# Fetching the output-projection matrix in runs of four rows per partition, with the attention output permuted to match

## Chip, cores, metric

One Trainium2 chip, one core. The metric is device time of one execution in microseconds (us). Repeated executions differ by up to 1.4 us in all (370.9 to 372.3 for the kernel before, in 11 runs of one set), so differences below 1 us need several rounds.

Names used below: PE is TensorE (matrix multiplies), DVE is VectorE, ACT is ScalarE, POOL is GpSimd, and SP is SyncE, which here issues loads. PSUM is the memory that PE writes to; `arena` is the kernel's one large SBUF buffer. A load is cut into packets, which 16 DMA engines carry.

## The reference

A gated sum of two branches on eight tokens: attention of one query position over a window of 2,048 cached positions, then an output projection, and a two-layer MLP.

```python
g = sigmoid((x * gate_w).sum(-1, keepdims=True))
q = (x @ wq).reshape(B, 1, 32, 128)                 # B = 8, D = 576
k, v = k_cache[:, :, -2048:], v_cache[:, :, -2048:] # 16 kv heads, each used by 2 query heads
o = softmax(q k^T / sqrt(128)) v
a = o.reshape(B, 1, 4096) @ wo                      # wo is 4096 x 576, bf16: 4.7 MB
b = gelu(layernorm(x) @ w1 + b1) @ w2 + b2          # F = 4608
out = g * a + (1 - g) * b
```

Keys and values are 134 MB of the 154 MB that must be read. `wo` is 3% of it.

## The kernel before

A plan of operations with dependencies is put in order once for each engine, on the host, and then emitted. SP issues nearly all loads into nine slots of 16 KB per partition. A key tile is transposed on DVE and multiplied on PE; a value tile goes straight to PE. After every eight query heads, one load brings the eight blocks of 128 rows of `wo` that belong to them. Row p of a block goes to partition p, so each partition gets eight separate runs of one row, 576 x 2 = 1,152 B.

```python
def wo_chunk(i):                                   # i = 0..3, eight heads each
    s = take_slot()
    h0 = WO_CH * i                                 # WO_CH = 8
    dst = slot(s)[:, 0:WO_CH * WOP].rearrange("p (t c) -> p t c", t=WO_CH)      # WOP = 768
    d = dma("sp", lambda e: e.dma_start(dst[:, :, 0:D],
            A_wo[128 * h0:128 * (h0 + WO_CH), :].rearrange("(t p) c -> p t c", p=128)), ...)
    for item in range(h0 // 2, (h0 + WO_CH) // 2):
        mms = [(oT[:, item, h, :], dst[:, 2 * item + h - h0, 0:D]) for h in range(2)]
        ops.append(AccGroup("proj%d" % item, mms, [oT_done[item], d], cost=0.5).op)
    ...
# AccGroup: for each (lhsT, rhs) two matmuls of 288 columns, added up in one PSUM bank.
# ... cut ...
stream += [("B", 0)] + [("M", i) for i in range(FC)]   # after the last wo load: b2, then w2 in four parts
def m2_chunk(ci):                                      # w2: 1296 KB a part, the last one in three pieces
    cuts = [0, 4, 7, 9] if ci == FC - 1 else [0, FJ]
    # ... cut ...
```

Of the kernel before, what the change touches and what calls it, by code (L numbers as in the profile page):

```python
# [6 lines left out]
BF = mybir.dt.bfloat16  # L7
F32 = mybir.dt.float32
ACTF = mybir.ActivationFunctionType
# [29 lines left out]
class _Plan:  # L39
# [10 lines left out]
    def add(self, eng, fn, deps=(), name=None, cost=0.1, after=(), prio=0):  # L50
        op = _Op(eng, fn, deps, name, cost, after=after, prio=prio)
        op.idx = len(self.all)
        self.all.append(op)
        return op

    def dma(self, eng, fn, semkey, nbytes, deps=(), name=None, after=(), prio=0):
        op = _Op(eng, fn, deps, name, self.DMA_ISSUE, after=after, is_dma=True, dma_sem=semkey, nbytes=nbytes, prio=prio)
        op.idx = len(self.all)
        self.all.append(op)
        return op  # L60
# [111 lines left out]
def build_kernel(nc, A_x, A_k_cache, A_v_cache, A_wq, A_wo, B_x, B_w1, B_b1, B_w2, B_b2, gate_w, out):  # L172
    B, Sq, D = A_x.shape
# [12 lines left out]
    FC, FJ = 4, 9  # L186
    FT = FC * FJ
    FCW = 128 * FJ
    WOP = 768
    NJ = 2  # L190
    WO_CH = 8
    JN = D // NJ
# [4 lines left out]
    with ExitStack() as es:  # L197
# [5 lines left out]
        def req(name, nelem, dt, align=64):  # L203
            sz = 2 if dt == BF else 4
            o = aoff[0] + ARENA_BASE
            o = (o + align - 1) // align * align - ARENA_BASE
            R[name] = (o, nelem, dt)
            aoff[0] = o + nelem * sz
# [34 lines left out]
        req("rg", 2 * 32, F32)  # L243
        req("o32", 2 * 16, F32)
        req("oT", Hkv * 16, BF)
        req("out_sb", JN, BF)
        req("PT", 2 * 2048, BF)
        req("P", 2048, BF)
# [11 lines left out]
        arena = es.enter_context(nc.sbuf_tensor("arena", [128, (aoff[0] + 1) // 2], BF))  # L260
        AST = _pst(arena)
        arena_f = arena.bitcast(F32)

        def aoffs(name):
            return R[name][0] // 2
# [4 lines left out]
        def view(name, parts=128):  # L270
            o, n, dt = R[name]
            a = arena[0:parts, o // 2: o // 2 + (n * (2 if dt == BF else 4)) // 2]
            if dt == F32:
                a = a.bitcast(F32)
            return a

        ident = view("ident")
        ones_bf = view("ones_bf")
        ones_f = view("ones_f")
# [20 lines left out]
        dsum = view("dsum")  # L300
# [2 lines left out]
        o32 = view("o32").rearrange("p (u m) -> p u m", u=2)  # L303
        oT = view("oT").rearrange("p (u h b) -> p u h b", u=Hkv, h=2)
        out_sb = view("out_sb")
        PT = view("PT").rearrange("p (g r m) -> p g r m", g=2, m=32)
        Pm = view("P")
        RAW = view("RAW")
# [6 lines left out]
        def slot(s):  # L315
            return RAW[:, s * SE:(s + 1) * SE]
# [7 lines left out]
        def col(i, parts=128):  # L324
# [3 lines left out]
        ps = es.enter_context(nc.psum_tensor("ps", [128, 8, 512], F32))  # L328
        PST = _pst(ps)
# [2 lines left out]
        BK_OS = (4, 5)  # L332
        BK_S = 6
        BK_ACC = 7

        eng_sems = {e: es.enter_context(nc.semaphore("sem_" + e)) for e in ENGS}
        dma_keys = ["x", "b", "b2", "wq", "w1", "out", "outb"] + ["s%d" % i for i in range(NSLOT)] + ["t%d" % i for i in range(4)]
# [3 lines left out]
        add, dma = P.add, P.dma  # L341
# [4 lines left out]
        o_ident = add("pool", lambda e: e.affine_select(out=ident, in_=ones_bf[:, 0:128], pattern=[[-1, 128]], compare_op=ALU.is_equal,  # L346
                                                        fill=0.0, base=0, channel_multiplier=1), deps=[o_ones], name="ident", cost=0.3)
# [33 lines left out]
        for s in range(2):  # L381
            o_xz.append(add("dve", (lambda s=s: lambda e: e.tensor_copy(xz[:, s, :].rearrange("p (k z) -> p k z", z=2)[:, :, s], x_sb[:, 512:576]))(),  # L382
                            deps=dx + [o_xz0], name="xz%d" % s, cost=0.12))
# [12 lines left out]
        for s in range(2):  # L396
            o_yz.append(add("dve", (lambda s=s: lambda e: e.tensor_copy(yz[:, s, :].rearrange("p (k z) -> p k z", z=2)[:, :, s], y_bf[:, 512:576]))(),
                            deps=[o_y, o_yz0], name="yz%d" % s, cost=0.12))
# [30 lines left out]
        def b1ev_fn(e):  # L429
# [5 lines left out]
                   deps=[o_dga, o_dgb, o_onesf], name="g_pe", cost=0.4, after=[o_yTp])  # L435
        o_yT = add("dve", ev_T(yT, 1), deps=[o_gp, o_yTp], name="yT_ev", cost=0.2)
        o_gb = add("dve", lambda e: e.tensor_copy(gb, ps[:, BK_X, 384:400]), deps=[o_gp], name="gb_ev", cost=0.15)
# [118 lines left out]
        exp_done, pt_done, pv_last = {}, {}, {}  # L556
        rg_done = {}
        o_item_ev = {}
        proj_ops = {}
        oT_done = {}  # L560

        def src_of(cache, g, q):
# [8 lines left out]
        def softmax(g):  # L571
            k = lambda i, n=1, parts=128, p0=0: sm[p0:p0 + parts, g, i:i + n]
            MX, GA, GB_, GC_, M01, M23, TT, NB, SUM, S = 0, 1, 2, 3, 4, 5, 6, 7, 8, 12
            mx = add("dve", lambda e: e.tensor_reduce(out=k(MX), in_=ps[:, 0:4, :].rearrange("p a n -> p (a n)"), axis=AXL.X, op=ALU.max), deps=[qk_unit[4 * g + 3]], name="mx%d" % g, cost=2.25, prio=5)  # L574
            sh = []
            for i, dst in ((1, GA), (2, GB_), (3, GC_)):
                sh.append(add("dve", (lambda i=i, dst=dst: lambda e: e.tensor_copy(k(dst, 1, 32), k(MX, 1, 32, 32 * i)))(), deps=[mx], name="mg%d_%d" % (g, i), cost=0.16, prio=5))  # L577
            m01 = add("dve", lambda e: e.tensor_tensor(out=k(M01, 1, 32), in0=k(MX, 1, 32), in1=k(GA, 1, 32), op=ALU.max), deps=[sh[0]], name="m01_%d" % g, cost=0.16, prio=5)
            m23 = add("dve", lambda e: e.tensor_tensor(out=k(M23, 1, 32), in0=k(GB_, 1, 32), in1=k(GC_, 1, 32), op=ALU.max), deps=sh[1:], name="m23_%d" % g, cost=0.16, prio=5)
            tt = add("dve", lambda e: e.tensor_tensor(out=k(TT, 1, 32), in0=k(M01, 1, 32), in1=k(M23, 1, 32), op=ALU.max), deps=[m01, m23], name="t_%d" % g, cost=0.16, prio=5)  # L580
            nbs = []
            for q in range(4):
                nbs.append(add("dve", (lambda q=q: lambda e: e.tensor_scalar(out=k(NB, 1, 32, 32 * q), in0=k(TT, 1, 32), scalar1=-SCALE, scalar2=None, op0=ALU.mult))(),  # L583
                               deps=[tt], name="nb%d_%d" % (g, q), cost=0.16, prio=5))
            exs = []
            for c in range(4):
                def fn(e, c=c):
                    return e.activation(out=Pm[:, 512 * c:512 * c + 512], in_=ps[:, c, :], func=ACTF.Exp, bias=k(NB), scale=SCALE, accum_out=k(SUM + c))  # L588
                exs.append(add("act", fn, deps=nbs + ([pt_done[g - 1][c]] if g else [o_xg, o_zz]), name="exp%d_%d" % (g, c), cost=0.9, prio=5))
            exp_done[g] = exs  # L590
            pts = []
            for c in range(4):
                pts.append(add("dve", (lambda c=c: lambda e: e.transpose(PT[:, g % 2, 16 * c:16 * c + 16, :].rearrange("p r m -> p (r m)"), Pm[:, 512 * c:512 * c + 512]))(),  # L593
                               deps=[exs[c]] + ([pv_last[g - 2]] if g >= 2 else [o_yTp, o_b1p]), name="pt%d_%d" % (g, c), cost=0.62, prio=5))
            pt_done[g] = pts
            s_ = add("dve", lambda e: e.tensor_reduce(out=k(S), in_=k(SUM, 4), axis=AXL.X, op=ALU.add), deps=exs, name="s_%d" % g, cost=0.16, prio=5)
            ds = add("dve", lambda e: e.tensor_scalar(out=dsum, in0=i32, scalar1=k(S), scalar2=None, op0=ALU.mult), deps=[s_] + o_i32 + ([rg_done[g - 1]] if g else []), name="ds_%d" % g, cost=0.16, prio=5)
            sp_ = add("pe", lambda e: e.matmul(ps[:, BK_S, 0:32], ones_f, dsum, start=True, stop=True), deps=[ds, o_yT, o_gb], name="sum_pe%d" % g, cost=0.5, prio=5)  # L598
            rc = add("dve", lambda e: e.reciprocal(out=rr, in_=ps[:, BK_S, 0:32]), deps=[sp_], name="rc_%d" % g, cost=0.16, prio=5)  # L599

            def rg_fn(e):
                in1 = bass.AP(arena_f, offset=foffs("gb"), ap=[[AST // 2, 128], [0, 2], [1, 8], [0, 2]])
                return e.tensor_tensor(out=rg[:, g % 2, :].rearrange("p (l b h) -> p l b h", l=2, b=8), in0=rr.rearrange("p (l b h) -> p l b h", l=2, b=8), in1=in1, op=ALU.mult)
            deps = [rc, o_gb]
            if g >= 2:
                deps.append(oT_done[2 * (g - 2) + 1])
            rg_done[g] = add("dve", rg_fn, deps=deps, name="rg_%d" % g, cost=0.16, prio=5)
# [81 lines left out]
        def wo_chunk(i):  # L689
            s = take_slot()  # L690
            h0 = WO_CH * i
            dst = slot(s)[:, 0:WO_CH * WOP].rearrange("p (t c) -> p t c", t=WO_CH)
            d = dma("sp", lambda e: e.dma_start(dst[:, :, 0:D], A_wo[128 * h0:128 * (h0 + WO_CH), :].rearrange("(t p) c -> p t c", p=128)),
                    "s%d" % s, WO_CH * 128 * D * 2, deps=slot_free[s], name="d_wo%d" % i, after=last_dma[-1:])
            last_dma.append(d)
            ops = []
            for item in range(h0 // 2, (h0 + WO_CH) // 2):
                mms = [(oT[:, item, h, :], dst[:, 2 * item + h - h0, 0:D]) for h in range(2)]
                ops.append(AccGroup("proj%d" % item, mms, [oT_done[item], d], cost=0.5).op)
            slot_free[s] = ops  # L700

        o_m2 = []
# [105 lines left out]
```

## Time and profile before

| | before |
|---|---|
| time, median of the first 3 runs | 372.0 us (371.48 to 372.11) |
| load queue, share of 16 DMA engines | 98.5% |
| PE / DVE / ACT / POOL busy | 65 / 57 / 8 / 10% |
| instruction fetches (queue 8) | 24, of 16,384 B each |

These are lines of the profile page of the kernel before. "DMA" gives the mean busy share of the 16 DMA engines in 40 equal slices, in tenths. The queue lines (q1, q8) give packets, megabytes, and share of the 16 engines' span. The line that starts with "DMA 6" is the chain of waits by engine. The last line is the issue of the projection loads: KB each, and us from issue to landing.

```profile
span 369.5 us, 7044 instructions
...
DMA  8999999999999999999999999999999999999994
...
DMA packets 14934, 154.77 MB, mean 419 GB/s; under 512 B 1292, under 2 KB 5428, under 8 KB 6072
...
q1 hardware_dynamic: 14848, 154.29, 98.5%
q8 instruction: 24, 0.39, 0.4%
...
DMA 63%; PE 20%; DVE 13%; SPq 2%; issue 1%; DVEq 0%
...
arena<-in_A_wo_dram SPq DMA_DIRECT2D x4, 1152.0 KB, 37.3
```

DMA is at 9 tenths everywhere but at the ends, so DMA engine time is what counts. PE, DVE and ACT have room.

How the rate sags where a projection load runs (208 to 212 us), against a stretch without one. The columns of this view: stretch; length; busy us (instructions) of PE, PE weight loads, DVE, ACT, POOL; granted clock; DMA share; GB/s.

```profile
208.00:212.00 4.00, 0.00 (x0) 0.00 (x1) 3.74 (x9) 2.78 (x8) 0.00 (x0) 0.68 0.98 383
150.00:196.00 46.00, 32.64 (x401) 17.95 (x406) 28.05 (x29) 3.16 (x11) 4.58 (x22) 0.80 1.01 430
```

383 GB/s against 430, at the same DMA share: small packets carry less.

The end of the kernel before, from its timeline: start us, duration us, engine, line, operation; in brackets the idle time before it and who ended it.

```profile
350.83 1.87 PE L663 MATMUL ps<-arena 128*128 128x8 bf16 x64 [2.97 <-DMA arena<-in_A_v_cache_dram]
352.74 0.23 DVE L685 TENSOR_TENSOR arena<-ps,arena 128x16 bf16<-128x16 f32 x1 [13.97 <-PE ps L663]
...
353.93 2.65 PE L530 MATMUL ps<-arena 128*8 128x288 bf16 x20 [1.23 <-DMA arena<-in_A_wo_dram]
...
357.10 2.33 PE L530 MATMUL ps<-arena 128*8 128x288 bf16 x18 [0.51 <-DMA arena<-in_B_w_dram]
...
360.06 2.33 PE L530 MATMUL ps<-arena 128*8 128x288 bf16 x18 [0.63 <-DMA arena<-in_B_w_dram]
...
363.15 3.96 PE L530 MATMUL ps<-arena 128*8 128x288 bf16 x36 [0.77 <-DMA arena<-in_B_w_dram]
```

L663 is the last value tile, L685 scales the attention output, and L530 holds the projection and then the second MLP layer. Each L530 line from 353.93 on begins when weights land: `wo` at 353.9, then three parts of `w2`; PE ends at 367.1.

The trace holds a record of each DMA packet: queue, size, start, duration. These durations are the same from the 5th to the 95th percentile (for the 256 packets of 4,608 B in the kernel before, 181 ns at the 95th):

| packet | duration in the record | from one packet's start to the next one's on the same engine |
|---|---|---|
| 1,152 B (`wo`) | 51 ns | 47 ns |
| 4,608 B | 178 ns | 174 ns |
| 16,384 B (K, V) | 611 ns | 607 ns |

### The profile page before, as it was taken

To read this page: it belongs to the slowest core of one execution; us is meant where nothing else is said; L and a number is where in the kernel's file an instruction comes from. 1 tells how busy PE (TensorE), PEld (TensorE's weight loads), DVE (VectorE), ACT (ScalarE), POOL (GpSimd) and SP (SyncE) were. 2 spreads that over 40 slices of the span, in tenths; PEclk is the share of its full clock that TensorE was granted. 3 is DMA by queue.
4 is the path that set the end of the run, shared out by engine and by line. 5 is a ranking of instruction groups with operands and counts; after the bars stand their busy time and mean duration, and the time that the engine had idled before them with its cause. 6 is when DMAs were issued, how large, how long until landed. Compare 5 with 4: busy or idle time off the path is not lost.

```text
span 369.5 us, 7044 instructions
## 1 busy us (share of the span) xinstructions
PE 242.0 (65%) x3089; PEld 137.5 (37%) x3117; DVE 210.0 (57%) x253; ACT 28.6 (8%) x85; POOL 37.5 (10%) x163
## 2 busy tenths in 40 slices
PE   0349983896695486663965395755767385783376
PEld 0339430454242243232523243432424243343343
DVE  0704699688694663459744764478544964464000
ACT  1010001100300200003000300003000300003000
POOL 7030010011011001000101010100101000000000
PEclk9999998799698879686898879696957788785556
DMA  8999999999999999999999999999999999999994
GB/s 343 426 422 424 427 432 431 434 424 431 429 431 429 413 436 427 429 427 429 435 426 429 414 431 432 431 431 426 426 435 433 418 424 427 435 429 426 413 420 167
DMA packets 14934, 154.77 MB, mean 419 GB/s; under 512 B 1292, under 2 KB 5428, under 8 KB 6072
## 3 DMA queue, kind: packets, MB, share of 16 engines
q1 hardware_dynamic: 14848, 154.29, 98.5%
q8 instruction: 24, 0.39, 0.4%
q14 instruction: 6, 0.05, 0.0%
q10 hardware_dynamic: 56, 0.03, 0.0%
HBM read 154.31 MB, written 0.01 MB: 418 GB/s over the span
## 4 chain that ended last, share of the span: by engine, by line
DMA 63%; PE 20%; DVE 13%; SPq 2%; issue 1%; DVEq 0%
DMA arena<-in_A_k_cache_dram 42%; PE ps L641 12%; DMA arena<-in_B_w_dram 11%; DMA arena<-in_A_v_cache_dram 10%; DVE arena L627 9%; PE ps L663 3%; DVE arena L574 2%; PE ps L487 2%; SPq L716 1%; PE ps L530 1%; PE ps L637 1%; SPq L657 1%; PE ps L489 1%; DVE arena L577 0%; DVE arena L593 0%
## 5 line engine op out<-in xcount | busy, mean ns | idle before, releaser
L627 DVE STREAM_TRANSPOSE arena<-arena 128x2048 f32<-128x2048 f32 x64 | 145.0, 2296 | 79.1 <-DMA arena<-in_A_k_cache_dram 74.6
L641 PE MATMUL ps<-arena 128*128 128x512 bf16 x491 | 144.6, 449 | 45.1 <-DVE arena L627 44.0
L641 PEld LDWEIGHTS ps<-arena 128*128 128x128 bf16 x512 | 52.5, 109 | 129.2 <-DVE arena L627 53.2
L663 PE MATMUL ps<-arena 128*128 128x8 bf16 x2048 | 56.4, 166 | 12.3 <-DMA arena<-in_A_v_cache_dram 12.3
L663 PEld LDWEIGHTS ps<-arena 128*128 128x128 bf16 x2048 | 56.1, 97 | 19.1 <-DMA arena<-in_A_v_cache_dram 14.2
L620 POOL COPY arena<-arena 32x32 bf16<-32x32 bf16 x128 | 26.0, 203 | 177.2 <-PE ps L641 162.6
L637 PE MATMUL ps<-arena 128*128 128x512 bf16 x25 | 12.3, 630 | 40.2 <-DVE arena L593 36.7
L588 ACT ACTIVATE arena<-ps,arena 128x512 bf16<-128x512 f32 x32 | 21.5, 685 | 107.4 <-DVE arena L583 107.4
L574 DVE TENSOR_REDUCE arena<-ps 128x1 f32<-128x2048 f32 x8 | 18.3, 2282 | 17.7 <-PE ps L641 17.7
L593 DVE STREAM_TRANSPOSE arena<-arena 128x512 bf16<-128x512 bf16 x32 | 19.9, 675 | 0.9 <-ACT arena L588 0.9
L637 PEld LDWEIGHTS ps<-arena 128*128 128x128 bf16 x32 | 3.5, 128 | 42.9 <-DVE arena L593 38.5
L530 PE MATMUL ps<-arena 128*8 128x288 bf16 (+1 forms) x140 | 14.7, 377 | 3.1 <-DMA arena<-in_B_w_dram 1.9
L685 POOL TENSOR_TENSOR arena<-arena 128x16 bf16<-128x16 f32 x15 | 4.0, 265 | 121.2 <-ACT arena L678 121.2
L678 ACT ACTIVATE arena<-ps 128x16 f32<-128x16 f32 x15 | 2.8, 184 | 170.2 <-PE ps L663 170.2
L487 PE MATMUL ps<-arena 128*128 128x8 bf16 x144 | 10.9, 201 | 4.6 <-DMA arena<-in_B_w_dram 4.6
L487 PEld LDWEIGHTS ps<-arena 128*128 128x128 bf16 x144 | 10.8, 160 | 5.0 <-DMA arena<-in_B_w_dram 5.0
L530 PEld LDWEIGHTS ps<-arena 128*8 128x8 bf16 (+1 forms) x140 | 7.1, 106 | 10.9 <-DMA arena<-in_B_w_dram 3.6
L599 DVE RECIPROCAL arena<-ps 128x32 f32<-128x32 f32 x8 | 2.9, 358 | 11.4 <-PE ps L598 11.4
L409 PE MATMUL ps<-arena 8*128 8x8 bf16 x8 | 0.5, 167 | 13.4 <-DVE arena L382 9.7
L734 DVE CAST arena<-ps 8x288 bf16<-8x288 f32 x1 | 0.4, 446 | 14.3 <-PE ps L530 14.3
L685 DVE TENSOR_TENSOR arena<-ps,arena 128x16 bf16<-128x16 f32 x1 | 0.2, 228 | 14.0 <-PE ps L663 14.0
L489 PE MATMUL ps<-arena 128*128 128x8 bf16 x36 | 7.2, 201 | 0.0
(79 smaller groups left out, 79.4 us busy)
## 6 DMA issues: line engine op xcount, KB each, us to landing
arena<-in_A_k_cache_dram SPq DMA_DIRECT2D x32, 2048.0 KB, 34.0
arena<-in_A_v_cache_dram SPq DMA_DIRECT2D x32, 2048.0 KB, 34.4
arena<-in_B_w_dram SPq DMA_DIRECT2D x1, 4608.0 KB, 24.2
arena<-in_A_wo_dram SPq DMA_DIRECT2D x4, 1152.0 KB, 37.3
arena<-in_A_wq_dram SPq DMA_DIRECT2D x1, 4096.0 KB, 13.0
arena<-in_B_w_dram SPq DMA_DIRECT2D x3, 1296.0 KB, 14.8
arena<-in_B_w_dram SPq DMA_DIRECT2D x2, 576.0 KB, 20.5
arena<-in_A_wq_dram SPq DMA_DIRECT2D x1, 512.0 KB, 3.6
```

The source lines that it names most:

```text
L487: ins = e.matmul(out_, lhsT, yT[:, kt, :], start=(kt == 0), stop=False)
L489: ins = e.matmul(out_, lhsT, yT[:, 4 + c // 2, :], start=False, stop=True)
L530: ins = e.matmul(ps[32 * j:32 * j + 8, BK_ACC, 0:JN], lhsT, rhs[:, JN * j:JN * j + JN], start=False, stop=True, skip_group_check=True, til ...
L574: mx = add("dve", lambda e: e.tensor_reduce(out=k(MX), in_=ps[:, 0:4, :].rearrange("p a n -> p (a n)"), axis=AXL.X, op=ALU.max), deps=[qk_ ...
L588: return e.activation(out=Pm[:, 512 * c:512 * c + 512], in_=ps[:, c, :], func=ACTF.Exp, bias=k(NB), scale=SCALE, accum_out=k(SUM + c))
L593: pts.append(add("dve", (lambda c=c: lambda e: e.transpose(PT[:, g % 2, 16 * c:16 * c + 16, :].rearrange("p r m -> p (r m)"), Pm[:, 512 * ...
L620: return e.tensor_copy(dst, src)
L627: tr = add("dve", (lambda h=h, kb=kb: lambda e: e.transpose(bass.AP(arena_f, offset=foffs("KT") + kb * 2048, ap=[[AST // 2, 128], [1, 2048]]),
L637: mm = e.matmul(ps[:, rc, :], maskL, maskR, start=True, stop=False)
L641: mm = e.matmul(ps[:, rc, :], qbd[:, ub, 2 * h + ee, :], rhs, start=False, stop=(q == 3 and h == 1 and ee == 1))
L663: mm = e.matmul(ps[:, BK_OS[item % 2], 8 * (q % 2):8 * (q % 2) + 8], slot(s)[:, r * 128:(r + 1) * 128], PT[:, g % 2, r, 8 * q:8 * q + 8], ...
L685: return e.tensor_tensor(out=oT[:, item, :, :].rearrange("p h b -> p b h"), in0=src_.rearrange("p (b h) -> p b h", h=2), in1=rg[:, g % 2, ...
```

## The change

The intent is to have fewer, longer DMA packets. Partition p takes four rows of `wo` that are neighbours in memory, 4p to 4p+3 of a group of 512 rows (four heads): one run of 4,608 B. The contraction on PE needs the attention output's rows on the same partitions. So for each load 16 matmuls with columns of the identity select and place them, and ACT copies the result from PSUM. The number of projection matmuls stays. Followed by hand, the indices pair each row of `wo` with its head and position. The cut parts of the diff put the permutation and the softmax sum, which share a PSUM bank, in order.

```diff
-    dst = slot(s)[:, 0:WO_CH * WOP].rearrange("p (t c) -> p t c", t=WO_CH)
-    d = dma("sp", lambda e: e.dma_start(dst[:, :, 0:D], A_wo[...].rearrange("(t p) c -> p t c", p=128)), ...)
+    dst = slot(s)[:, 0:WO_CH * D]
+    d = dma("sp", lambda e: e.dma_start(dst.rearrange("p (g n) -> p g n", g=2),
+            A_wo[...].rearrange("(g p t) c -> p g (t c)", g=2, t=4)), ...)
+    def perm_fn(e):
+        for hh in range(4):
+            rhs = bass.AP(arena, offset=aoffs("oT") + 8 * (h0 + hh), ap=[[AST, 128], [32, 2], [1, 8]])
+            for t in range(4):
+                out_ = bass.AP(ps, offset=32 * hh * PST + BK_S * 512 + WC + 8 * t, ap=[[PST, 32], [32, 2], [1, 8]])
+                lhsT = bass.AP(arena, offset=aoffs("ident") + t, ap=[[AST, 128], [4, 32]])
+                mm = e.matmul(out_, lhsT, rhs, start=True, stop=True, skip_group_check=True, tile_position=(0, 32 * hh))
+        return mm
+    pm = add("pe", perm_fn, deps=[oT_done[h0 // 2 + k] for k in range(4)] + ..., name="perm%d" % i, cost=1.0)
+    pe_ = add("act", lambda e: e.activation(out=w8, in_=ps[:, BK_S, WC:WC + 64], func=ACTF.Copy), deps=[pm] + ...)
-    for item in range(h0 // 2, (h0 + WO_CH) // 2):
-        mms = [(oT[:, item, h, :], dst[:, 2 * item + h - h0, 0:D]) for h in range(2)]
-        ops.append(AccGroup("proj%d" % item, mms, [oT_done[item], d], cost=0.5).op)
+    for n in range(2):
+        mms = [(w8[:, 8 * c:8 * c + 8], dst[:, c * D:(c + 1) * D]) for c in range(4 * n, 4 * n + 4)]
+        ops.append(AccGroup("proj%d_%d" % (i, n), mms, [pe_, d], cost=1.0).op)
```

More of the change, by code (lines that the diff above doesn't have):

```diff
@@ L188, in build_kernel @@
     FCW = 128 * FJ
-    WOP = 768
     NJ = 2
@@ L245, in build_kernel @@
         req("oT", Hkv * 16, BF)
+        req("wo8", 2 * 64, BF)
         req("out_sb", JN, BF)
@@ L305, in build_kernel @@
         out_sb = view("out_sb")
+        wo8 = view("wo8").rearrange("p (u n) -> p u n", u=2)
         PT = view("PT").rearrange("p (g r m) -> p g r m", g=2, m=32)
@@ L334, in build_kernel @@
         BK_ACC = 7
+        WC = 128
         eng_sems = {e: es.enter_context(nc.semaphore("sem_" + e)) for e in ENGS}
@@ L558, in build_kernel @@
         o_item_ev = {}
-        proj_ops = {}
+        b6_w, b6_r = [], [o_yT, o_gb]
+        wo_ops = {}
         oT_done = {}
@@ L597, in softmax @@
             ds = add("dve", lambda e: e.tensor_scalar(out=dsum, in0=i32, scalar1=k(S), scalar2=None, op0=ALU.mult), deps=[s_] + o_i32 + ([rg_done[g - 1]] if g else []), name="ds_%d" % g, cost=0.16, prio=5)
-            sp_ = add("pe", lambda e: e.matmul(ps[:, BK_S, 0:32], ones_f, dsum, start=True, stop=True), deps=[ds, o_yT, o_gb], name="sum_pe%d" % g, cost=0.5, prio=5)
+            sp_ = add("pe", lambda e: e.matmul(ps[:, BK_S, 0:32], ones_f, dsum, start=True, stop=True), deps=[ds] + b6_r[-2:], after=b6_w[-1:], name="sum_pe%d" % g, cost=0.5, prio=5)
+            b6_w.append(sp_)
             rc = add("dve", lambda e: e.reciprocal(out=rr, in_=ps[:, BK_S, 0:32]), deps=[sp_], name="rc_%d" % g, cost=0.16, prio=5)
+            b6_r.append(rc)
             def rg_fn(e):
@@ L691, in wo_chunk @@
             h0 = WO_CH * i
-            dst = slot(s)[:, 0:WO_CH * WOP].rearrange("p (t c) -> p t c", t=WO_CH)
-            d = dma("sp", lambda e: e.dma_start(dst[:, :, 0:D], A_wo[128 * h0:128 * (h0 + WO_CH), :].rearrange("(t p) c -> p t c", p=128)),
+            dst = slot(s)[:, 0:WO_CH * D]
+            d = dma("sp", lambda e: e.dma_start(dst.rearrange("p (g n) -> p g n", g=2), A_wo[128 * h0:128 * (h0 + WO_CH), :].rearrange("(g p t) c -> p g (t c)", g=2, t=4)),
                     "s%d" % s, WO_CH * 128 * D * 2, deps=slot_free[s], name="d_wo%d" % i, after=last_dma[-1:])
             last_dma.append(d)
+            def perm_fn(e):
+                mm = None
+                for hh in range(4):
[5 more added lines that the diff above has]
+                return mm
+            pm = add("pe", perm_fn, deps=[oT_done[h0 // 2 + k] for k in range(4)] + [o_ident] + b6_r[-2:], after=b6_w[-1:], name="perm%d" % i, cost=1.0)
+            b6_w.append(pm)
+            w8 = wo8[:, i % 2, :]
+            pe_ = add("act", lambda e: e.activation(out=w8, in_=ps[:, BK_S, WC:WC + 64], func=ACTF.Copy), deps=[pm] + wo_ops.get(i - 2, []), name="pev%d" % i, cost=0.25, prio=3)
+            b6_r.append(pe_)
             ops = []
-            for item in range(h0 // 2, (h0 + WO_CH) // 2):
-                mms = [(oT[:, item, h, :], dst[:, 2 * item + h - h0, 0:D]) for h in range(2)]
-                ops.append(AccGroup("proj%d" % item, mms, [oT_done[item], d], cost=0.5).op)
+            for n in range(2):
+                mms = [(w8[:, 8 * c:8 * c + 8], dst[:, c * D:(c + 1) * D]) for c in range(4 * n, 4 * n + 4)]
+                ops.append(AccGroup("proj%d_%d" % (i, n), mms, [pe_, d], cost=1.0).op)
+            wo_ops[i] = ops
             slot_free[s] = ops
```

## The prediction

> **What bounds the kernel now.** The DMA engines. The page's slice table shows DMA at 9 tenths in all slices but the first and last; the queue table puts the load queue at 98.5% of the 16 engines' span (154.29 MB, 14,848 packets). In the chain of waits DMA is 63%. Loads are issued about 34 us before they land (DMA issues table), so work is always queued. PE (65%) and DVE (57%) are not at their limit. What counts is DMA engine time, plus the short tail after the last landing.
>
> **What the change removes.** Each of the four projection loads (1152 KB) is 1,024 packets of 1,152 B. The trace's packet records give 51 ns for 1,152 B, 178 ns for 4,608 B, 611 ns for 16,384 B. A straight line through the last two has 8.6 ns of fixed time per packet and predicts 51.0 ns for 1,152 B. This agrees in kind with the Trainium skill, "DMA: Bandwidth & Descriptors", section "Why small descriptors are slow (HBM only)", which states a fixed overhead per packet. Runs of four rows make 256 packets per load: 48 fewer per engine, x 8.6 ns = 0.41 us per load, 1.65 us for four. The windows agree: in 208 to 212 us, where the second of these loads runs, the rate is 370 to 399 GB/s, against 430 in 150 to 196 us.
>
> Section "How a descriptor splits into AXI transactions" says that an unaligned start costs extra beats; every second 1,152 B row starts off a 256 B boundary, yet the records show 51 ns from the 5th to the 95th percentile. I expect nothing extra from alignment.
>
> **What it adds.** Per load: 16 selection matmuls (the MLP stage's strided-weight matmuls follow each other every 60 ns in the chain: estimate 1.0 us), one ACT copy (0.18 us for the similar 128x16 eviction) and two semaphore hops: about 1.4 us of latency. Projection matmuls stay 16 per load. For the first three loads this is off the critical path, with loads queued some 30 us ahead: 0. Fewer packets should shorten the long load issue that follows each projection load (20 to 26 us in the sync engine's timeline), but the DMA engines weren't idle then: 0.
>
> **The tail.** Before: last value load lands at 350.8, output scaled at 353.0, projection weights land at 353.9, projection and bias matmuls (20, 2.65 us) until 356.6, three MLP weight landings at 357.1, 360.1, 363.15, PE until 367.1. After: landings move up 1.2 us (1.65 after the fourth load). Scaled output 351.7, permutation and copy to 353.1, projection and bias to 355.7, next landing 355.5: at worst 0.3 us late, and PE has 0.6 to 0.8 us idle before each following landing to absorb it. Cost 0 to 0.2 us.
>
> **Prediction.** 372.0 - 1.65 + 0.1 = 370.4 us, a gain of 0.4%. Range 369.3 to 371.6. Faster by over 2%: 0.01; within 2%: 0.98; slower by over 2%: 0.01.
>
> **What would show each step.** Packets fall by about 3,072, those under 2 KB from 5,428 to about 1,330. New 4,608 B packets take 178 ns. The rate dip at the projection loads at least halves. The last MLP weight landing and the span come about 1.6 us earlier. ACT gains four copies of about 0.2 us, PE 64 matmuls; in the tail the projection waits for the ACT copy instead of the weights.
>
> **What would make it wrong.** A PE order in which a permutation waits for a late output and holds up scores, so that DVE frees slots late and the load queue runs dry. An extra instruction fetch on the same DMA engines. Or the slowest DMA engines set the end (some finish about 4 us after the others) and lag for a cause that this change alters.

## More of the kernel before

The records don't name the engine. A packet was put on the engine whose previous packet ended where it starts; the commonest distance from end to next start was -4 ns, that is, neighbours overlap by 4 ns. From one packet's start to the next one's on the same engine: 47 ns for 1,152 B (`wo`), 174 ns for 4,608 B, 607 ns for 16,384 B (K, V).

## The result, and the profile after

| | before | after |
|---|---|---|
| median (4 runs each, same rounds) | 371.74 us (371.33 to 372.11) | 371.73 us (371.44 to 372.09) |
| ratio | | 1.000 (0.9986 to 1.0014) |

A ratio here is the mean time of one kernel's runs over that of the other's of the same rounds, so not quite the ratio of the medians quoted. The brackets after a ratio are its 95% interval. The time didn't move, to within 0.5 us.

Lines of the profile page of the kernel after:

```profile
span 369.7 us, 7204 instructions
...
DMA  8999999999999999999999999999999999999992
...
DMA packets 11863, 154.78 MB, mean 419 GB/s; under 512 B 1292, under 2 KB 1332, under 8 KB 3000
...
q1 hardware_dynamic: 11776, 154.29, 98.0%
q8 instruction: 25, 0.41, 0.4%
...
DMA 67%; PE 19%; DVE 12%; issue 1%; SPq 0%; ACT 0%; DVEq 0%
...
arena<-in_A_wo_dram SPq DMA_DIRECT2D x4, 1152.0 KB, 36.0
```

The packets did fall as intended: 3,071 fewer in all, those under 2 KB from 5,428 to 1,332, and the load queue's share from 98.5% to 98.0%. But q8 went from 24 fetches to 25. The rate in the same two stretches, columns as before:

```profile
208.00:212.00 4.00, 0.00 (x0) 0.00 (x0) 3.68 (x11) 2.37 (x7) 0.00 (x0) 0.86 0.99 417
150.00:196.00 46.00, 35.78 (x406) 18.52 (x406) 27.90 (x29) 3.34 (x11) 4.62 (x23) 0.75 1.01 430
```

The sag at the projection load is mostly gone: 417 GB/s instead of 383. The end of the kernel after, from its timeline:

```profile
350.16 1.87 PE L668 MATMUL ps<-arena 128*128 128x8 bf16 x64 [2.98 <-DMA arena<-in_A_v_cache_dram]
352.07 0.23 DVE L690 TENSOR_TENSOR arena<-ps,arena 128x16 bf16<-128x16 f32 x1 [14.03 <-PE ps L668]
...
352.45 0.34 PE L709 MATMUL ps<-arena 128*32 128x16 bf16 x16 [0.41 <-DVE arena L690]
352.86 0.22 ACT L714 ACTIVATE arena<-ps 128x64 bf16<-128x64 f32 x1 [10.36 <-PE ps L709]
...
352.94 2.66 PE L532 MATMUL ps<-arena 8*8 8x288 bf16 x20 [0.15 <-DMA arena<-in_B_b_dram]
...
356.02 2.04 PE L532 MATMUL ps<-arena 128*8 128x288 bf16 x18 [0.42 <-DMA arena<-in_B_w_dram]
...
359.11 1.27 PE L532 MATMUL ps<-arena 128*8 128x288 bf16 x18 [1.05 <-DMA arena<-in_B_w_dram]
...
363.50 3.79 PE L532 MATMUL ps<-arena 128*8 128x288 bf16 x36 [3.12 <-DMA arena<-in_B_w_dram]
```

The permutation (L709) takes 0.34 us and the copy (L714) 0.22 us. Bias and projection (the first L532 line) start at 352.9, a microsecond earlier than before. The next two weight landings, 356.02 and 359.11, are 1.1 and 1.0 us ahead of 357.10 and 360.06. The third comes at 363.50, after 363.15. A gain of 1 us was there at 359 us, and it was gone four microseconds later.

Stretches of 1 us at the end show why. First the kernel before, then the kernel after; the last two columns are the DMA share and GB/s.

```profile
362.00:363.00 1.00, 0.38 (x4) 0.00 (x0) 0.00 (x0) 0.00 (x0) 0.00 (x0) 0.50 0.58 239
363.00:364.00 1.00, 0.85 (x8) 0.49 (x10) 0.00 (x0) 0.00 (x0) 0.00 (x0) 0.50 0.53 219
364.00:365.00 1.00, 1.00 (x12) 0.53 (x8) 0.00 (x0) 0.00 (x0) 0.00 (x0) 0.50 0.53 215
365.00:366.00 1.00, 1.00 (x12) 0.54 (x10) 0.00 (x0) 0.00 (x0) 0.00 (x0) 0.50 0.38 146
366.00:367.00 1.00, 1.00 (x14) 0.52 (x10) 0.00 (x0) 0.00 (x0) 0.00 (x0) 0.79 0.00 0
```

```profile
362.00:363.00 1.00, 0.00 (x0) 0.00 (x0) 0.00 (x0) 0.00 (x0) 0.00 (x0) 1.00 0.53 220
363.00:364.00 1.00, 0.50 (x10) 0.37 (x11) 0.00 (x0) 0.00 (x0) 0.00 (x0) 1.00 0.52 211
364.00:365.00 1.00, 1.00 (x16) 0.45 (x12) 0.00 (x0) 0.00 (x0) 0.00 (x0) 0.73 0.43 167
365.00:366.00 1.00, 1.00 (x10) 0.33 (x8) 0.00 (x0) 0.00 (x0) 0.00 (x0) 0.50 0.06 24
366.00:367.00 1.00, 1.00 (x12) 0.25 (x10) 0.00 (x0) 0.00 (x0) 0.00 (x0) 0.50 0.01 5
```

A share of 0.53 means that about half of the 16 engines still work. Before, that half stops within the stretch 365 to 366 and nothing is left from 366 on. After, the share falls to 0.06 in that stretch, and 0.06 is one engine of sixteen (1/16 = 0.0625), at 24 GB/s. All the others have finished, and the last pieces of `w2` wait for one.

The packet records say when each engine finished the last load (the last piece of `w2`, 128 packets of 2,304 B, eight to an engine). Packets of one engine follow each other every 89 to 90 ns here, and by this spacing the 128 fall into 16 trains of eight. Of the eight fastest engines, only the first is given.

| | first to end | the eight slowest |
|---|---|---|
| before | 361.34 | 365.60, 365.78, 365.80, 365.80, 365.83, 365.84, 365.85, 365.96 |
| after | 360.37 | 364.71, 364.81, 364.82, 364.85, 364.88, 364.93, 365.00, **366.21** |

Rank by rank, fifteen engines gained 0.5 to 1.3 us (the seven not listed included), and seven of the slow eight 0.85 to 0.98. The last lost 0.25 us. The third part of `w2`, whose landing starts PE's last work, shows the same: after, its last packet on the slowest engine ended at 363.03, on the others by 361.82, and PE started at 363.50; before, the slowest ended at 362.78 and PE started at 363.15. In the packet records the 25th instruction fetch starts at 359.7 us. Around the earlier fetches the records show the same picture: the fetch packet and the load packet that follows it on its engine take 0.9 and 1.1 us instead of 0.61 each, and that engine's own loads come 1.41 us later from then on (the median over a kernel's fetches; 607 ns for the fetch itself, and about 315 and 490 ns that the two packets take over 607). Eight faster engines (361.3 to 363.6 us in the kernel before) and eight slow ones (365.6 to 366.0), the first of each 4.3 us apart, fit 24 fetches dealt out to eight engines, three each: 3 x 1.41 = 4.2 us. The fetch packets' own durations point the same way: they repeat with a period of eight (before, from the second on: 936, 938, 922, 964, 962, 954, 881, 878 ns, then 935, 938, 928, 962, 962, 949, 879, 879); in each of the nine runs, fetches eight apart differ by 2 to 6 ns in the median, fetches one to seven apart by 7 to 53.

One caution on the tail: in the profile after, PE was granted full clock from 361 to 364 us, against half in the profile before. The engine ends above don't depend on it; PE's last microsecond does, by some tenths. At half clock PE takes 3.9 to 4.5 us for its last 36 matmuls (before and e1 to e5), and the timeline shows their weight loads in one stretch with no wait listed in between, so there the slowest engine sets the end through the landing of the third part. In the profile after, PE waits for the pieces too: its weight loads stood idle for 0.42, 0.48 and 0.38 us until one landed. The profiles of all experiments had half clock from 362 to 366 us, as before.

### The profile page after: what moved, and what is told of

The parts are those of the page before. It is cut to its first block, busy times and chain, and to the rows that moved or that the text cites. A ratio compares the mean times of both kernels' runs of the same rounds, so it can differ in the third digit from the quotient of the medians. Undisturbed runs are those within 1.5% of the kernel's fastest.

```text
span 369.7 us, 7204 instructions
## 1 busy us (share of the span) xinstructions
PE 252.0 (68%) x3181; PEld 140.2 (38%) x3181; DVE 209.8 (57%) x253; ACT 29.5 (8%) x89; POOL 37.5 (10%) x163
## 2 busy tenths in 40 slices
DMA packets 11863, 154.78 MB, mean 419 GB/s; under 512 B 1292, under 2 KB 1332, under 8 KB 3000
## 3 DMA queue, kind: packets, MB, share of 16 engines
q1 hardware_dynamic: 11776, 154.29, 98.0%
## 4 chain that ended last, share of the span: by engine, by line
DMA 67%; PE 19%; DVE 12%; issue 1%; SPq 0%; ACT 0%; DVEq 0%
DMA arena<-in_A_k_cache_dram 51%; DMA arena<-in_B_w_dram 16%; PE ps L646 11%; DVE arena L632 10%; PE ps L668 3%; PE ps L489 2%; PE ps L642 1%; PE ps L532 1%; DVE arena L577 1%; PE ps L491 1%; DVE arena L596 0%; DVE arena L586 0%; DVE arena L580 0%; DVE arena L755 0%; SPq L377 0%
## 5 line engine op out<-in xcount | busy, mean ns | idle before, releaser
L646 PE MATMUL ps<-arena 128*128 128x512 bf16 x512 | 154.0, 460 | 35.9 <-DVE arena L632 35.9
L646 PEld LDWEIGHTS ps<-arena 128*128 128x128 bf16 x512 | 54.1, 111 | 124.3 <-issue 44.5
L668 PEld LDWEIGHTS ps<-arena 128*128 128x128 bf16 x2048 | 56.5, 97 | 16.5 <-DMA arena<-in_A_v_cache_dram 11.3
L642 PE MATMUL ps<-arena 128*128 128x512 bf16 x32 | 14.9, 620 | 38.7 <-DVE arena L596 34.8
L642 PEld LDWEIGHTS ps<-arena 128*128 128x128 bf16 x32 | 3.5, 127 | 44.0 <-DVE arena L596 39.6
L532 PE MATMUL ps<-arena 128*8 128x288 bf16 (+1 forms) x140 | 13.2, 344 | 5.9 <-DMA arena<-in_B_w_dram 4.6
L489 PEld LDWEIGHTS ps<-arena 128*128 128x128 bf16 x144 | 10.8, 160 | 5.1 <-DMA arena<-in_B_w_dram 5.1
L532 PEld LDWEIGHTS ps<-arena 128*8 128x8 bf16 (+1 forms) x140 | 6.0, 95 | 11.9 <-DMA arena<-in_B_w_dram 7.1
```

The source lines that it names most:

```text
L489: ins = e.matmul(out_, lhsT, yT[:, kt, :], start=(kt == 0), stop=False)
L532: ins = e.matmul(ps[32 * j:32 * j + 8, BK_ACC, 0:JN], lhsT, rhs[:, JN * j:JN * j + JN], start=False, stop=True, skip_group_check=True, til ...
L642: mm = e.matmul(ps[:, rc, :], maskL, maskR, start=True, stop=False)
L646: mm = e.matmul(ps[:, rc, :], qbd[:, ub, 2 * h + ee, :], rhs, start=False, stop=(q == 3 and h == 1 and ee == 1))
L668: mm = e.matmul(ps[:, BK_OS[item % 2], 8 * (q % 2):8 * (q % 2) + 8], slot(s)[:, r * 128:(r + 1) * 128], PT[:, g % 2, r, 8 * q:8 * q + 8], ...
```

## The experiments

The theory after the first look, called the fetch theory: the longer packets save 0.9 us, less than predicted, and PE's 128 added instructions (64 matmuls and 64 weight loads) pull in one more 16 KB block of instructions, on a DMA engine that finishes last anyway, which takes it back. The rivals: the permutation's latency in the tail eats the gain; the longer packets save nothing; every added instruction costs in proportion. Each kernel was timed in five rounds beside the kernel before on the same chip, four kernels in a first set and three in a second. The diffs are shortened; `...` and names in angle brackets stand for what was cut. The Trainium skill's page "Runtime: NRT & Kernel Launch", section "Instruction fetch mechanics", states that an engine's instructions are refilled in 16 KiB blocks of 256 and that the sequencer drives its own DMA queue for it. The size of the q8 packets agrees, and so does their number: 24 for 2 x 3,117 PE matmul and weight-load instructions (6,234 / 256 = 24.4; PE has a few others, so the exact boundary isn't known).

### e1_pad_before: the cost without the benefit

```diff
+    def pad_fn(e):
+        for _ in range(64):
+            mm = e.matmul(ps[0:32, 3, 0:8], zeros_bf[:, 0:32], zeros_bf[:, 0:8], start=True, stop=True, ...)
+        return mm
+    o_pad = add("pe", pad_fn, deps=[o_z], name="pad", cost=3.0, after=[o_gp], prio=9)   # ahead of the query projection
```

> The kernel before with 64 dummy matmuls put into PE's stream at the start, where PE waits for the query weights; nothing else. It adds 128 PE instructions, as many as the permutation does. Fetch theory (the change's gain is eaten by a 25th 16 KB instruction fetch on one of the eight DMA engines that already finish last): 25 fetches instead of 24, one DMA engine ends 1.2 us later, time 0.9 to 1.3 us above before (about 372.8). Rival 1 (the permutation's own latency in the tail eats the gain): no change, within 0.3 us. Rival 2 (the packets save nothing): no change.

Measured: 372.85 us (372.57 to 373.22) against 371.62 (370.86 to 372.25) before; ratio 1.0036 (1.0024 to 1.0049). From its profile, the fetch queue and the stretches at the end:

```profile
q8 instruction: 25, 0.41, 0.4%
```

```profile
365.00:366.00 1.00, 1.00 (x12) 0.58 (x10) 0.00 (x0) 0.00 (x0) 0.00 (x0) 0.50 0.37 144
366.00:367.00 1.00, 1.00 (x12) 0.58 (x10) 0.00 (x0) 0.00 (x0) 0.00 (x0) 0.50 0.06 24
```

Again one engine alone, one stretch later than in the kernel after. PE's last work (before: 363.15) starts as much later:

```profile
364.52 3.89 PE L537 MATMUL ps<-arena 128*8 128x288 bf16 x36 [2.19 <-DMA arena<-in_B_w_dram]
```

64 matmuls of no use, put where PE idles 350 us before the end, cost 1.3 us: the ends are 365.81 for the second last engine and 367.23 for the last. They stand nowhere near the tail, so what they cost isn't their own time. The fetch theory holds, and both first rivals, which expected no change, don't explain it.

### e2_load_only: the benefit without the cost

```diff
-    mms = [(w8[:, 8 * c:8 * c + 8], dst[:, c * D:(c + 1) * D]) for c in range(4 * n, 4 * n + 4)]
+    mms = [(oT[:, (h0 + c) // 2, c % 2, :], dst[:, c * D:(c + 1) * D]) for c in range(4 * n, 4 * n + 4)]
```
(and the permutation and the copy are cut out)

> The new four-row load alone, projection fed with the unpermuted output (the result is wrong on purpose), no permutation and no copies. Fetch theory: 24 fetches, 3,072 fewer packets, and a gain by the spacing of packets in the trace (47 ns for 1,152 B, 174 ns for 4,608 B) of 64 x 47 - 16 x 174 = 224 ns per load, 0.9 us for four: about 370.8. The prediction's sizing by packet durations: 1.65 us, about 370.1. Rival 1 (permutation latency): 370.1. Rival 2 (packets save nothing): 371.7.

Measured: 370.59 us (369.88 to 371.37), ratio 0.9973 (0.9957 to 0.9988), so 0.4 to 1.6 us faster. 24 fetches; the slowest engine ended at 365.21, 0.75 us before the 365.96 of the kernel before. The load alone is worth about 0.9 us, as the spacing of the packets says (4 x 224 ns); the 1.65 us of the prediction lies just outside the interval, and above what the engine ends show. That the packets save nothing is ruled out. The result is wrong on purpose and yet passed the comparison, so its tolerance doesn't see this part of the sum: passing it says nothing of the permutation.

### e3_four_wide: the whole change with fewer instructions

```diff
-            for hh in range(4): ... for t in range(4): ...        # 16 matmuls into 32 partitions each
+            for t in range(4):                                    # sel[:, t, 32*hh + i] = ident[:, 4*i + t]
+                mm = e.matmul(ps[:, BK_S, WC + 64 * t:WC + 64 * t + 64], sel[:, t, :], oT_of_eight_heads, start=True, stop=True, ...)
-            activation(out=w8, in_=ps[:, BK_S, WC:WC + 64], func=Copy)
+            for hh in range(4): activation(out=w8[32 * hh:32 * hh + 32, :] ..., in_=<heads hh and hh + 4 of that block>, func=Copy)
```
(the selection matrix is built by four POOL copies, in a buffer no longer in use)

> The changed kernel with the permutation done by 4 full-width selection matmuls and 4 ACT copies per eight heads in place of 16 and 1; right result. 24 fewer PE instructions per load, so only 32 more than before. Fetch theory: 24 fetches, 0.9 us faster than before, about 370.8. Rival 1 (latency of the permutation): its latency is longer by three copies of 0.2 us, so no faster than the changed kernel, 371.7 or above.

Measured: 370.70 us (370.20 to 370.94), ratio 0.9974 (0.9962 to 0.9987). The time was as expected, one statement in the expectation wasn't: this kernel has 25 fetches too. The 25th comes at 364.8 us, when the loads are all but through, as its stretches show:

```profile
364.00:365.00 1.00, 1.00 (x12) 0.57 (x10) 0.00 (x0) 0.00 (x0) 0.00 (x0) 0.50 0.47 167
365.00:366.00 1.00, 1.00 (x12) 0.57 (x10) 0.00 (x0) 0.00 (x0) 0.00 (x0) 0.50 0.01 2
```

0.47 and then 0.01: there is no engine left over. The slowest ended at 365.09, and PE's last work started 0.8 us earlier than before (363.15):

```profile
362.35 4.27 PE L539 MATMUL ps<-arena 128*8 128x288 bf16 x36 [0.79 <-DMA arena<-in_B_w_dram]
```
So it isn't the number of fetches alone that matters, but whether a load still has to pass behind the last of them on that engine. This is the whole change with the permutation in place (its indices, too, work out by hand), and it is 0.5 to 1.4 us faster than the kernel before. The kernel after wasn't timed in the same rounds; it stood at 1.000 (0.9986 to 1.0014) to the kernel before. The rival by which the permutation's latency eats the gain falls, since the latency here is three copies longer.

### e4_pad_after: a step or a slope

The same 64 dummy matmuls as in e1, put into the kernel after.

> The changed kernel with the same 64 dummy matmuls at the start. Fetch theory: 25 fetches as without them (the next block of 256 instructions isn't reached), so the same time as the changed kernel, within 0.3 us of before: the cost is a step, not a slope. Rival 3 (every PE instruction added costs DMA time in proportion): about 1 us slower than before.

Measured: 372.01 us (371.33 to 372.60), ratio 1.0011 (0.9998 to 1.0024). 25 fetches, the last at 355.1 us; the last engine ended at 366.26 (kernel after: 366.21), the second last at 365.25 (365.00). By the ratio it is 0.4 us above before (-0.1 to 0.9), a little more than the 0.3 that was expected but not clear of it; by the last engine's end, another 128 instructions cost 0.05 us, where the first 128 cost 1.3. A step then, within what can be told; a slope of 1 us per 128 instructions lies outside the interval only just, but the engine ends speak against it, and e6 below far more so: 1,960 instructions for 1.5 us.

### e5_last_only: the narrow form kept where it stands in the tail

```diff
+    if i == 3:                      # the 16 selection matmuls and the copy, as in the changed kernel
         ...
+    else: pe_ = None                # the first three loads take the unpermuted output
```

> The changed kernel with its 16 narrow selection matmuls and the copy kept only for the last eight heads, where they stand in the tail; the first three loads use the unpermuted output (wrong result on purpose). 96 fewer PE instructions than the changed kernel, the same number as the four-wide version, so the 25th fetch should come at about 364 us, too late to hold up a load. Fetch theory: about 0.9 us faster than before, as the four-wide version. Rival (the narrow form of the permutation in the tail costs the gain, and the four-wide form doesn't): no faster than before.

Measured: 370.64 us (370.00 to 371.15) against 371.55 (370.93 to 372.11); ratio 0.9973 (0.9958 to 0.9987). The 25th fetch came at 365.7 us and the slowest engine ended at 365.34. The narrow permutation, in the only place where its latency could show, costs nothing measurable. With e3, this leaves the instruction count as the difference between the kernel after and those that gain.

### e6_fetch32 and e7_fetch33: how fetches are dealt out

```diff
     def pv_fn(e):
+        for _ in range(35 if i < 28 else 0):        # e7: 41
+            e.matmul(ps[0:32, BK_ACC, 300:308], zeros_bf[:, 0:32], zeros_bf[:, 0:8], start=True, stop=True, ...)
```

> The kernel before with 35 dummy matmuls ahead of each of the first 28 value-tile groups: 1,960 PE instructions more, to reach 32 fetches and not the 33rd. If fetches go round eight of the sixteen DMA engines in turn, 24 is three on each, 25 to 32 is four on the unluckiest: the same cost as the 128 dummy instructions, 1.2 us above before (0.9 to 1.6). If each fetch costs in proportion to its number, 8 fetches cost about 8 times the first: 5 us or more; if they spread evenly over all engines, about 0.5 us.

> The same with 41 dummy matmuls each: 2,296 PE instructions more, to reach the 33rd fetch. Round eight engines: one engine has five, 2.4 us above before (2.0 to 2.8), a step of 1.2 us against the run with 32 fetches. No step (less than 0.4 us) if fetches aren't dealt out in turn.

Measured against the same 371.55 us: e6 373.24 us (372.60 to 373.88), ratio 1.0041 (1.0027 to 1.0055); e7 374.48 us (373.83 to 374.58), ratio 1.0074 (1.0061 to 1.0087). The fetch queue of e6, then of e7:

```profile
q8 instruction: 32, 0.52, 0.5%
```

```profile
q8 instruction: 33, 0.54, 0.5%
```

One fetch more than before cost 1.3 us (e1), eight more 1.5, nine more 2.7: steps at the 25th and the 33rd, and hardly anything between. This fits dealing out to eight engines in turn, and not to sixteen, where the 25th would have made no step, nor to four, where a step would have come at the 29th. In e7 one engine ended at 368.65, the next at 367.34; in e6 none ends alone (the slow eight at 367.1 to 367.9), as four fetches on each of eight would have it. Something isn't clean in e6 and e7: the fast engines also ended later than before, the first to end by 2.2 and 1.7 us (363.54 and 363.03). The load queue ran dry once, with 4 to 5 engine-microseconds idle between 345 and 352 us (before: none there), and the first `w2` packets of 10,368 B after it took up to 1.3 us instead of 0.39. The added PE work seems to free the slots of the last value tiles later; that wasn't tested. So the 1.5 and 2.7 us against before may hold some of this; the difference between e6 and e7, which share it, and the one engine that ends alone in e7 rest on firmer ground.

### Summary

| run | fetches | last fetch at | slowest engine ends | ratio to before |
|---|---|---|---|---|
| before | 24 | 355.0 | 365.96 | 1 |
| after | 25 | 359.7 | 366.21 | 1.000 |
| e1 dummies on before | 25 | 360.7 | 367.23 | 1.0036 |
| e2 new load only | 24 | 354.5 | 365.21 | 0.9973 |
| e3 four wide matmuls | 25 | 364.8 | 365.09 | 0.9974 |
| e4 dummies on after | 25 | 355.1 | 366.26 | 1.0011 |
| e5 permutation in tail only | 25 | 365.7 | 365.34 | 0.9973 |
| e6 | 32 | 359.8 | 367.92 | 1.0041 |
| e7 | 33 | 356.7 | 368.65 | 1.0074 |

## Why the prediction was wrong

It said 370.4 us with a range of 369.3 to 371.6, and the kernel took 371.73. Point by point:

- **What bounds the kernel**: right. DMA engine time. But the mean share hid that the engines aren't alike: half of them end some 4 us after the others, and the last one sets the time. The prediction named this as a danger and put no number on it.
- **"8.6 ns of fixed time per packet ... 0.41 us per load, 1.65 us for four"**: the mechanism was right, the size wrong by nearly two. The durations in the records overlap by 4 ns from packet to packet. By the spacing, the fixed time is 4.6 ns (174 ns less 4,608 B at the slope of 433 ns for 11,776 B), and a load saves 64 x 47 - 16 x 174 = 224 ns, four save 0.90 us. e2 measured 0.4 to 1.6 us by its interval, and 0.75 us by the slowest engine's end.
- **Alignment adds nothing**: the records agree, 47 ns from start to start for nearly all rows, whether or not they begin on a 256 B boundary.
- **"For the first three loads this is off the critical path ... : 0" and "Cost 0 to 0.2 us" in the tail**: right for the permutation's latency. e3 and e5 show that it costs nothing measurable, and 16 matmuls took 0.34 us in the tail where 1.0 was estimated.
- **The failed step**: the sum "372.0 - 1.65 + 0.1". It counted what the added instructions take on PE and ACT, and not that they have to be fetched through the same DMA engines. "An extra instruction fetch on the same DMA engines" stands in the prediction as something that could make it wrong, with a weight of zero in the sum. It put the last engine 1.2 us behind the next in the kernel after (e1: 1.3 us of time by itself). Against a true saving of 0.9 us that leaves about nothing, and the ratio, known to 0.5 us either way, says nothing more than that. The mis-sized saving alone would have left a gain (e2: 1.0 us); the fetch that was left out took it.
- **The long load issue after a projection load**, 20 to 26 us, did shrink, as predicted; that this was worth nothing wasn't tested by itself. From the sync engine's timelines, before and then after (start us, duration us):

```profile
95.53 0.59 SPq L693 DMA_DIRECT2D arena<-in_A_wo_dram  x1
105.85 20.47 SPq L612 DMA_DIRECT2D arena<-in_A_k_cache_dram  x1
```

```profile
96.59 0.59 SPq L698 DMA_DIRECT2D arena<-in_A_wo_dram  x1
107.09 0.54 SPq L617 DMA_DIRECT2D arena<-in_A_k_cache_dram  x1
```

That only eight of the 16 engines carry fetches, and in turn, is inferred from steps, end times and the period of eight in the fetches' durations; the records don't name the engine.

## What to carry to other kernels

Where the DMA engines are full, instructions are load too: count the blocks of 256 that a change adds on the busiest instruction stream, and look at when the last block is fetched, because one fetch can make one engine late and a load completes with its slowest engine (here 363.03 us, against 361.82 for the others). Where the added work can be done with fewer PE instructions, as in e3 (32 instead of 128), the gain comes back. Judge a packet's cost by the distance from start to start, since recorded durations may overlap. A mean share of 98% doesn't tell whether sixteen engines are busy to the end or eight; read the last microseconds in short stretches.

## What the Trainium skill lacked or had wrong

- "Runtime: NRT & Kernel Launch", section "Instruction fetch mechanics", calls the cost of crossing a 16 KiB boundary "one DMA tail-bump, mostly hidden". Here the DMA side of it isn't hidden: a fetch puts the loads of one of the 16 DMA engines back by 1.41 us, and the 25th fetch cost 1.3 us of the kernel's time (e1), the 33rd another 1.2 (e7 against e6).
- The same section doesn't say over which DMA engines the fetches go. The runs fit eight of the 16 in turn: steps at the 25th and the 33rd fetch, and two groups of eight engines ending some 4 us apart (361.3 and 365.6 us for the first of each, in the kernel before), and a period of eight in the fetches' durations (2 to 6 ns between fetches eight apart).
- "DMA: Bandwidth & Descriptors", section "Why small descriptors are slow (HBM only)", gives an overhead per packet but not how profile records show it: the recorded durations are 4 ns longer than the spacing (51 against 47 ns, 178 against 174, 611 against 607), so that durations overstate the fixed part, 8.6 ns against 4.6.
- Section "How a descriptor splits into AXI transactions" of that page says that an unaligned start costs beats; for rows of 1,152 B, at least every second one unaligned, the spacing shows nothing of it (47 ns at the 5th and the 75th percentile, 48 at the 95th).
